# Decay attention feeding experts and a mish FFN: scores on two row halves of the array, state update by heads, tokens counted one step back

## The chip, the cores and the metric

One Trainium2 chip, of which the program uses one core. The metric is device time in microseconds (us). The engines are TensorE (PE, matmuls; its weight loads are listed as PEld), VectorE (DVE), ScalarE (ACT), GpSimd (POOL) and SyncE (SP, which here issues most DMAs). A trace gives busy spans and what each instruction waited for; L393 is line 393 of the kernel.

## What is computed

Three layers in a row, on 1536 tokens of 512 numbers, all float32. First a causal attention with a decay per head (2 sequences, 8 heads, 768 positions, head size 64), in its blocked form:

```python
for b in range(nb):
    intra = np.einsum('bhic,bhjc->bhij', qb, kb) * Dmask[None]
    intra = np.einsum('bhij,bhjd->bhid', intra, vb)
    inter = np.einsum('bhid,bhde->bhie', qb * lam_pow[None], kv_state)
    out[:, :, sl] = intra + inter
    kv_state = lam_block * kv_state + np.einsum('bhsd,bhse->bhde', kb * rev_pow, vb)
```

Then 8 experts, one for each token: the largest of 8 logits picks it, and its softmax probability weighs the token's result (relu MLP, 512 to 1024 to 512). Last a dense FFN, 512 to 2048 to 512, with h * tanh(softplus(h)) between.

## The kernel before

The attention runs as 12 steps (STEPS): 6 blocks of 128 positions, for each of the 2 sequences in turn. All engines' instructions stand in program order, which the Python loop `for i in range(NS)` (L553) writes out by hand; nothing reorders them. Iteration i of the loop does, in this order:

- load_step(i + 2): q and k transposed (qbd, k_t), k and v as they are (k_n, v_n), 256 KB each, by SP's queue, three buffers each;
- scores(i + 1): the score block a on PE (L393), then DVE's product pt with the decay table dec (L397);
- factors(i + 1) on POOL: kd, which is k by decay (L409), and qs, which is q by powers of lam (L415, L416); fade(i) on ACT: the old state faded (sl, L424);
- rows(i - 1): the attention output xt of the step before, turned into token rows r with 8 logits beside them (L474); pick(i - 1): the largest logit, its index, the one-hot oh_all (L501), the exponentials and their sum (L504);
- the low half of one expert weight piece on DVE (low, L194). A weight piece (128 x 1024) is split for the experts into a rounded high part (hi, ACT, L189) and the remainder (lo, DVE or POOL, L194);
- values(i): o, from the old state and qs (L433) and from v and pt (L442), is copied to xt by ACT (L446); u, the update of the state (L451); then place(i - 1): counts of tokens per expert in c on PE (L510, L511), the gate gt (L513, L514), the weighed rows xs on ACT (L517, L521), the slot of each token (jk, obs, slot_i, L523 to L527), and a scatter of the rows to the experts' bins by POOL (L533);
- update(i): DVE adds u to the faded state (L465);
- in iterations 1 to 8: the load and high half of the next weight piece (its low half comes an iteration later).

q lies in memory that is zero elsewhere: for each pair of heads the first head's q is on rows 0 to 63 of one half of qbd, the second's on rows 64 to 127 of the other half, so one matmul with the pair's k (128 rows) and 256 columns gives both heads' scores.

```python
PE.matmul(
    out=a[:, j, :].rearrange("p (a i) -> p a i", a=2), lhsT=k_t[:, hp, :], rhs=q[:, :, hp, :],
    start=True, stop=True)
```

A float32 matmul stands in the trace as two records, each with a weight load of its own. After the loop the last tokens are placed, and the first expert's tokens are put together directly on PE (spread, gather). Then come the experts (up, L719; down, L740 and L743; between them hh, L722 and L723; further splits by advance), and the FFN.

Of the kernel before, what the change touches and what calls it, by code (L numbers as in the profile page):

```python
# [11 lines left out]
F32 = mybir.dt.float32  # L12
# [48 lines left out]
def kernel(  # L61
# [58 lines left out]
    eps = const.tile([P, 1], F32, name="eps")  # L120
# [44 lines left out]
    with tc.manual_schedule():  # L165
# [104 lines left out]
        with ExitStack() as actx:  # L270
            ap = actx.enter_context(pool("attn"))

            qbd = []
            for i in range(3):
                t = ap.tile([P, 2, NP, P], F32, name=f"qbd{i}")
                qbd.append(t)
            DVE.memset(qbd[0][HD:P, 0], 0.0)
            DVE.memset(qbd[0][0:HD, 1], 0.0)
            for t in qbd[1:]:
                POOL.memset(t[0:HD, 1], 0.0)  # L280
                POOL.memset(t[HD:P, 0], 0.0)

# [41 lines left out]

            dec = ap.tile([P, NH, P], F32, name="dec")
            pw = ap.tile([P, NP, P], F32, name="pw")
# [4 lines left out]
            def decay(g):  # L331
                h = slice(4 * g, 4 * g + 4)
                DVE.tensor_copy(out=sc0[:, h, :], in_=lam_b[:, h].unsqueeze(2).to_broadcast([P, 4, P]))
# [5 lines left out]
            def powers():  # L339
                DVE.tensor_copy(out=sc0[:, 0:NP, :], in_=lam_p.unsqueeze(2).to_broadcast([P, NP, P]))  # L340
# [19 lines left out]
            POOL.memset(eps, 1e-9)  # L360
# [18 lines left out]
            pt, qs, kd, xt, sld, rk, us, direct = {}, {}, {}, {}, {}, {}, {}, {}  # L379
            NS = len(STEPS)  # L380

            def scores(i):
                if i >= NS:
                    return
                q, k_t, k_n, v_n = ld[i]
                n = STEPS[i][0]
                for g in range(2):
                    if i == 0:
                        decay(g)
                    a = ps.tile([P, 2, 2 * P], F32, tag="a", name=f"a{i}_{g}", bufs=3)  # L390
                    for j in range(2):
                        hp = 2 * g + j
                        PE.matmul(  # L393
                            out=a[:, j, :].rearrange("p (a i) -> p a i", a=2), lhsT=k_t[:, hp, :], rhs=q[:, :, hp, :],
                            start=True, stop=True)
                    t = ap.tile([P, 4, P], F32, tag="pt", name=f"pt{i}_{g}", bufs=4)
                    DVE.tensor_tensor(  # L397
                        out=t.rearrange("p h i -> p (h i)"), in0=a.rearrange("p h i -> p (h i)"),
                        in1=dec[:, 4 * g:4 * g + 4, :].rearrange("p h i -> p (h i)"), op=ALU.mult)
                    pt[i, g] = t  # L400

            def factors(i):
# [4 lines left out]
                if n < NCH - 1:  # L407
# [3 lines left out]
                        in1=dec[:, :, P - 1:P].to_broadcast([P, NH, HD]), op=ALU.mult)  # L411
# [15 lines left out]
            def values(i):  # L427
# [10 lines left out]
                for h in range(NH):  # L438
                    if h == NH // 2 and i == NS - 2:
                        place(i - 1)  # L440
# [3 lines left out]
                        rhs=pt[i, hp // 2][:, h % 4, :], start=(n == 0 and hp == 0), stop=True, skip_group_check=True)  # L444
# [3 lines left out]
                if n < NCH - 1:  # L448
                    u = us[i] = ps.tile([P, NP, P], F32, tag="u", name=f"u{i}", bufs=1)
                    for hp in range(NP):  # L450
                        PE.matmul(  # L451
                            out=u[:, hp, :], lhsT=kd[i][:, 2 * hp:2 * hp + 2, :].rearrange("p h d -> p (h d)"),
                            rhs=v_n[:, hp * P:(hp + 1) * P], start=True, stop=True)
                if 1 <= i < NS - 2:
                    place(i - 1)

            def update(i):
                n, b = STEPS[i]
                if n < NCH - 1:
                    for z in range(2):  # L460
                        r = slice(z * HD, (z + 1) * HD)
                        if n == 0:
                            DVE.tensor_copy(out=state[b][r, :, r], in_=us[i][r, :, r])
                        else:
                            DVE.tensor_tensor(  # L465
                                out=state[b][r, :, r], in0=us[i][r, :, r], in1=sld[i][r, :, r], op=ALU.add)
# [21 lines left out]
            def pick(i):  # L488
# [9 lines left out]
                DVE.tensor_scalar(out=nm, in0=m8[:, 0:1], scalar1=-1.0, scalar2=None, op0=ALU.mult)  # L498
# [6 lines left out]
                rk[i] = (rv, sm)  # L505

            def place(i):
                rv, sm = rk.pop(i)
                c = ps.tile([P, NE], F32, tag="c", name=f"c{i}", bufs=1)
                PE.matmul(out=c, lhsT=tri[:, 1, :], rhs=obs, start=True, stop=False)  # L510
                PE.matmul(out=c, lhsT=tri[:, 0, :], rhs=oh_all[:, i, :], start=False, stop=True)  # L511
# [3 lines left out]
                xs = ap.tile([P, NP, P], F32, tag="xs", name=f"xs{i}", bufs=2)  # L515
# [491 lines left out]
```

## Time and profile before

| | |
|---|---|
| median of 3 runs (lowest to highest) | 542.11 us (541.7 to 542.39) |
| profiled execution: time, span | 541.75 us, 540.1 us |
| PE busy, share of the span | 522.6 us, 97% |
| PEld | 451.4 us, 84% |
| DVE | 369.8 us, 68% |
| ACT | 324.7 us, 60% |
| POOL | 185.2 us, 34% |
| granted TensorE clock, mean | 0.994 |

The shares are averages over three stages. The attention loop ends at about 85 us, the experts follow, then the FFN. A busy PE need not be a PE at its peak, since the ends of matmuls are modelled; the distance between the starts of blocks tells more.

### The profile page before, as it was taken

Reading aid. Unit: us, or ns where it says so; the run is one execution under the profiler, and the core shown is the slowest. Engines: PE = TensorE matmul, PEld = TensorE weight load, DVE = VectorE, ACT = ScalarE, POOL = GpSimd, SP = SyncE. Lnnn points to the kernel's source line nnn. Section 1 sums busy time; section 2 is a strip of 40 time slices with the busy share of each in tenths; the row PEclk is TensorE's granted clock in tenths of the full one; section 3 lists DMA queues with packets and bytes.
Section 4 is the critical chain, followed back from the end, with each engine's and each line's share of the span. In section 5 each row is a group of like instructions: output and inputs, shape, how many; then the busy total and the mean of one; then the engine's idle time right before and its main releaser. Section 6 shows DMA issues by size and latency. Waiting matters only on the chain. (4 is left out here: it accounts for less than half of the span.)

```text
span 540.1 us, 8441 instructions
## 1 busy us (share of the span) xinstructions
PE 522.6 (97%) x3101; PEld 451.4 (84%) x3102; DVE 369.8 (68%) x668; ACT 324.7 (60%) x514; POOL 185.2 (34%) x151
## 2 busy tenths in 40 slices
PE   8999988999999999999999999999999999999993
PEld 5888878999999999999788878888888888888882
DVE  7999965765967858653498776567965778436362
ACT  1566533655674566555678876777666775765650
POOL 7788842755573331235100321003210031103032
PEclk9999999999999999999999999999999999999997
DMA  8999837119999996731301024020230000001022
GB/s 259 340 329 332 277 147 292 52 49 399 315 299 224 223 360 236 262 128 40 118 0 62 18 79 133 23 79 0 95 139 4 0 0 1 0 1 58 21 80 81
DMA packets 28944, 74.98 MB, mean 139 GB/s; under 512 B 6652, under 2 KB 6652, under 8 KB 28896
## 3 DMA queue, kind: packets, MB, share of 16 engines
q1 hardware_dynamic: 25040, 66.62, 38.3%
q0 software_dynamic: 3424, 7.23, 3.6%
q8 instruction: 26, 0.43, 0.4%
q10 hardware_dynamic: 432, 0.53, 0.3%
q14 instruction: 22, 0.18, 0.1%
HBM read 66.61 MB, written 10.49 MB: 143 GB/s over the span
## 5 line engine op out<-in xcount | busy, mean ns | idle before, releaser
L194 POOL TENSOR_TENSOR lo_f<-w,hi_f 128x1024 fp32r<-128x1024 f32 x16 | 39.8, 2487 | 185.9 <-ACT hi_f L189 155.1
L719 PE MATMUL h<-x,hi_w 128*128 128x232 f32 x512 | 87.5, 274 | 0.0
L740 PE MATMUL y<-hh,hi_w 128*128 128x464 f32 x256 | 84.8, 380 | 0.9 <-DVE hh L723 0.9
L796 PE MATMUL hp<-yt,hi_f 128*128 128x512 f32 x256 | 79.3, 391 | 0.0
L719 PEld LDWEIGHTS h<-x,hi_w 128*128 128x128 f32 x512 | 77.8, 192 | 0.0
L828 PE MATMUL acc<-hi_f,ghi 128*128 128x512 f32 x192 | 76.2, 397 | 0.4 <-ACT Y L833 0.4
L828 PE MATMUL acc<-hi_f,glo 128*128 128x512 f32 x192 | 75.8, 395 | 0.0
L828 PE MATMUL acc<-lo_f,ghi 128*128 128x512 f32 x192 | 75.7, 394 | 0.0
L136 DVE TENSOR_TENSOR t<-t,hp 128x512 f32<-128x512 f32 x48 | 32.8, 684 | 61.1 <-ACT t L135 61.1
L719 PE MATMUL h<-x,lo_w 128*128 128x232 f32 x256 | 71.1, 278 | 0.0
L743 PE MATMUL y<-hh,lo_w 128*128 128x232 f32 x256 | 69.1, 270 | 0.0
L194 DVE TENSOR_TENSOR lo_w<-raw,hi_w 128x1024 fp32r<-128x1024 f32 x50 | 63.0, 1283 | 7.5 <-ACT hi_w L189 6.9
L132 ACT ACTIVATE t<-hp 128x512 f32<-128x512 f32 x48 | 28.6, 600 | 62.4 <-PE hp L796 62.1
L189 ACT ACTIVATE hi_w<-raw 128x1024 fp32r<-128x1024 f32 x64 | 64.5, 1055 | 0.9 <-DMA raw<-in_w1p_dram 0.9
L194 POOL TENSOR_TENSOR lo_w<-raw,hi_w 128x1024 fp32r<-128x1024 f32 x14 | 35.1, 2510 | 71.5 <-ACT hi_w L189 70.8
L796 PEld LDWEIGHTS hp<-yt,hi_f 128*128 128x128 f32 x256 | 48.1, 188 | 11.1
L740 PEld LDWEIGHTS y<-hh,hi_w 128*128 128x128 f32 x256 | 48.2, 188 | 6.1 <-DVE hh L723 1.1
L796 PE MATMUL hp<-yt,lo_f 128*128 128x512 f32 x128 | 50.4, 394 | 0.0
L719 PEld LDWEIGHTS h<-x,lo_w 128*128 128x128 f32 x256 | 49.0, 191 | 0.5
L743 PEld LDWEIGHTS y<-hh,lo_w 128*128 128x128 f32 x256 | 48.9, 191 | 0.0
L722 ACT ACTIVATE hh<-h 128x464 fp32r<-128x464 f32 x32 | 17.8, 558 | 49.7 <-PE h L719 45.2
L723 DVE SCALAR_TENSOR_TENSOR hh<-h,hh 128x464 fp32r<-128x464 f32 x32 | 20.4, 639 | 34.8 <-ACT hh L722 34.8
(163 smaller groups left out, 1032.9 us busy)
## 6 DMA issues: line engine op xcount, KB each, us to landing
raw<-in_w1p_dram SPq DMA_DIRECT2D x32, 512.0 KB
raw<-in_w2p_dram SPq DMA_DIRECT2D x32, 512.0 KB
w<-in_w3p_dram SPq DMA_DIRECT2D x32, 512.0 KB
xw<-bins SPq DMA_DIRECT2D x7, 512.0 KB
qbd<-in_qT_dram SPq DMA_DIRECT2D x24, 128.0 KB
v_n<-in_vN_dram SPq DMA_DIRECT2D x12, 256.0 KB
k_n<-in_kN_dram SPq DMA_DIRECT2D x10, 256.0 KB
k_t<-in_kT_dram SPq DMA_DIRECT2D x10, 256.0 KB
```

Source lines behind the costliest of these rows:

```text
L132: yield lambda: ACT.activation(out=t, in_=h, func=AF.Tanh, scale=0.5)
L136: yield lambda: DVE.tensor_tensor(out=t, in0=t, in1=h, op=ALU.mult)
L189: ACT.activation(out=hi, in_=r, func=AF.Copy)
L194: engine.tensor_tensor(out=lo, in0=r, in1=hi.bitcast(F32), op=ALU.subtract)
L719: PE.matmul(out=p[:, m, :], lhsT=w[:, s], rhs=x[k // 2][:, k % 2, r, :], start=(k == 0 and m == 0 and z == 0), stop=(k == KD - 1 and z == ...
L722: ACT.activation(out=h[:, :, 0, :], in_=p, func=AF.Relu)
L723: DVE.scalar_tensor_tensor(out=h[:, :, 1, :], in0=p, scalar=0.0, in1=h[:, :, 0, :].bitcast(F32), op0=ALU.max, op1=ALU.subtract)
L740: PE.matmul(out=y.rearrange("p z n -> p (z n)"), lhsT=whi[:, s], rhs=h[:, f].rearrange("p z n -> p (z n)"), start=(c == 0 and f == 0), sto ...
L743: PE.matmul(out=y[:, 1, :], lhsT=wlo[:, s], rhs=h[:, f, 0, :], start=False, stop=(c == 3 and f == 1), skip_group_check=True)
L796: PE.matmul(out=p, lhsT=w[:, s], rhs=x, start=(k == 0 and z == 0), stop=(k == KD - 1 and z == 2))
L828: PE.matmul(out=acc[t], lhsT=x[:, s], rhs=w[:, DM:2 * DM], start=(first and z == 0), stop=(last and z == 2))
```

## The change

- q is loaded as it is, in one DMA, without the zeroed halves (which six memsets had cleared). The scores of a pair of heads are two matmuls: the first head on rows 0 to 63, the second on rows 64 to 127, each 128 columns, into two score tiles, one for each place in the pair. The decay table is ordered by place in the pair to match. POOL's sum of the two halves of q (L415) goes.
- The state update u is computed by heads: 8 matmuls of 64 by 64 instead of 4 of 128 by 128, of which only the diagonal blocks were used.
- place is split in three: weigh (gate and xs), locate (c, jk, obs, slot_i) and scatter. weigh(i - 1) stands ahead of values(i); locate and scatter come one step later, for i - 2, behind the next scores and the next factors.
- The negation nm and the addition of 1e-9 to the sum go from DVE to ACT. kd reads the last column of the decay table from a copy (last).
- Weight pieces are split in iterations 3 to 8 instead of 1 to 8; the two that are missing are split when the experts begin. Iterations 9 and 10 load three pieces each instead of two.

```diff
             def load_qk(i, queue):
-                q = qbd[i % 3]
+                q = ap.tile([P, NP, P], F32, tag="q", name=f"q{i}", bufs=3)
                 k_t = ap.tile([P, NP, P], F32, tag="k_t", name=f"k_t{i}", bufs=3)
                 queue.dma_start(out=k_t, in_=kT[i])
-                SP.dma_start(out=q[0:HD, 0], in_=qT[i, 0:HD])
-                SP.dma_start(out=q[HD:P, 1], in_=qT[i, HD:P])
+                SP.dma_start(out=q, in_=qT[i])
...
             def powers():
+                DVE.tensor_copy(
+                    out=last.rearrange("p (h z) -> p h z", z=2),
+                    in_=dec.rearrange("p (z h) i -> p h z i", z=2)[:, :, :, P - 1])
...
-                for g in range(2):
+
+                a = [ps.tile([P, NP, P], F32, tag="a", name=f"a{i}_{z}", bufs=3) for z in range(2)]
+                for hp in range(NP):
+                    for z in range(2):
+                        r = slice(z * HD, (z + 1) * HD)
+                        PE.matmul(out=a[z][:, hp, :], lhsT=k_t[r, hp, :], rhs=q[r, hp, :], start=True, stop=True)
+                for z in range(2):
                     if i == 0:
-                        decay(g)
-                    a = ps.tile([P, 2, 2 * P], F32, tag="a", name=f"a{i}_{g}", bufs=3)
...
                 if n > 0:
                     s = ap.tile([P, NP, P], F32, tag="qs", name=f"qs{i}", bufs=2)
-                    POOL.tensor_tensor(out=s, in0=q[:, 0], in1=q[:, 1], op=ALU.add)
-                    POOL.tensor_tensor(out=s, in0=s, in1=pw, op=ALU.mult)
+                    POOL.tensor_tensor(out=s, in0=q, in1=pw, op=ALU.mult)
...
-                    u = us[i] = ps.tile([P, NP, P], F32, tag="u", name=f"u{i}", bufs=1)
-                    for hp in range(NP):
+                    u = us[i] = ps.tile([P, NP, HD], F32, tag="u", name=f"u{i}", bufs=1)
+                    for h in range(NH):
+                        hp, z = divmod(h, 2)
                         PE.matmul(
-                            out=u[:, hp, :], lhsT=kd[i][:, 2 * hp:2 * hp + 2, :].rearrange("p h d -> p (h d)"),
-                            rhs=v_n[:, hp * P:(hp + 1) * P], start=True, stop=True)
-                if 1 <= i < NS - 2:
-                    place(i - 1)
+                            out=u[z * HD:(z + 1) * HD, hp, :], lhsT=kd[i][:, h, :],
+                            rhs=v_n[:, h * HD:(h + 1) * HD], start=True, stop=True)
...
-                DVE.tensor_scalar(out=nm, in0=m8[:, 0:1], scalar1=-1.0, scalar2=None, op0=ALU.mult)
+                ACT.activation(out=nm, in_=m8[:, 0:1], func=AF.Copy, scale=-1.0)
...
-                DVE.tensor_scalar(out=gt, in0=sm, scalar1=eps[:, 0:1], scalar2=None, op0=ALU.add)
+                ACT.activation(out=gt, in_=sm, func=AF.Copy, bias=1e-9)
...
                 scores(i + 1)
+                if 2 <= i < NS - 1:
+                    locate(i - 2)
                 if i == 0:
                     powers()
                     factors(0)
                 factors(i + 1)
+                if 2 <= i < NS - 1:
+                    scatter(i - 2)
                 fade(i)
...
                 late = []
+                if 1 <= i < NS - 1:
+                    weigh(i - 1)
                 values(i)
+                if i == NS - 2:
+                    locate(i - 1)
+                    scatter(i - 1)
                 if i == 0:
                     constants()
                 update(i)
-                if 1 <= i <= 8:
+                if 3 <= i <= 8:
                     p, r = next_raw()
                     pieces[p] = high(r, f"w{p}")
                     late.append((p, r))
                 if i in (9, 10):
-                    for _ in range(2):
+                    for _ in range(3):
                         load_piece()
```

How the instructions stand on three engines, in iteration 6 of the loop. A row is a line, an operation and its tiles; the first number in a tile's name is the step it belongs to.

PE before: the scores a7, the rows r5, the output o6 (old state, then values), the update u6, the counts c5.

```order
L393 MATMUL a7_0_700<-qbd1_108,k_t7_603 128x256 x2
L393 MATMUL a7_1_705<-qbd1_108,k_t7_603 128x256 x2
L474 MATMUL r5_0_720<-rw_151,xt5_664 128x136 x3
L474 MATMUL r5_1_721<-rw_151,xt5_664 128x136
L433 MATMUL o6_740<-qs6_623,state0_158 128x128 x4
L442 MATMUL o6_740<-pt6_0_614,v_n6_518 64x128 x4
L442 MATMUL o6_740<-pt6_1_619,v_n6_518 64x128 x4
L451 MATMUL u6_755<-v_n6_518,kd6_621 128x128 x4
L510 LDWEIGHTS tri_63
L510 MATMUL c5_760<-obs_67,tri_63 128x8
L511 LDWEIGHTS tri_63
L511 MATMUL c5_760<-oh_all_66,tri_63 128x8
```

PE with the change: the first three rows are the last of eight score matmuls of step 7, and the last two the first of eight value matmuls of step 6, behind which the eight of u6 follow.

```order
L385 MATMUL a7_0_718<-q7_612,k_t7_613 128x128
L385 MATMUL a7_1_719<-q7_612,k_t7_613 128x128
L511 LDWEIGHTS tri_63
L511 MATMUL c4_732<-obs_67,tri_63 128x8
L512 LDWEIGHTS tri_63
L512 MATMUL c4_732<-oh_all_66,tri_63 128x8
L463 MATMUL r5_0_749<-rw_141,xt5_690 128x136 x3
L463 MATMUL r5_1_750<-rw_141,xt5_690 128x136
L425 MATMUL o6_775<-qs6_643,state0_149 128x128 x4
L432 MATMUL o6_775<-pt6_0_630,v_n6_518 64x128
L432 MATMUL o6_775<-pt6_1_632,v_n6_518 64x128
```

The scores alternate between two tiles, and the counts have moved from behind u to behind the scores, for the token tile one step further back.

DVE before, from the one-hot of tile 5 to the first logits of tile 6 (obs is the running count, dec the decay table):

```order
L501 TENSOR_SCALAR oh_all_66<-iota8_64,i85_733 128x8
L194 TENSOR_TENSOR lo_w4_690<-raw4_509,hi_w4_689 128x1024
L513 TENSOR_SCALAR gt5_763<-sm5_737,eps_90 128x1
L514 RECIPROCAL gt5_763<-gt5_763 128x1
L523 SCALAR_TENSOR_TENSOR jk5_769,slot_f_68<-c5_760,oh_all_66 128x8
L526 TENSOR_TENSOR obs_67<-obs_67,oh_all_66 128x8
L527 CAST slot_i_69<-slot_f_68 128x1
L465 TENSOR_TENSOR state0_158<-u6_755,sl6_715 64x4x64 x2
L397 TENSOR_TENSOR pt8_0_792<-a8_0_789,dec_153 128x512
L397 TENSOR_TENSOR pt8_1_797<-a8_1_794,dec_153 128x512
L492 TENSOR_REDUCE lg6_815<-r6_0_809 128x8
```

DVE with the change, between the same two places:

```order
L490 TENSOR_SCALAR oh_all_66<-iota8_64,i85_762 128x8
L193 TENSOR_TENSOR lo_w2_708<-raw2_607,hi_w2_707 128x1024
L500 RECIPROCAL gt5_768<-gt5_768 128x1
L454 TENSOR_TENSOR state0_149<-u6_790,sl6_744 64x4x64 x2
L390 TENSOR_TENSOR pt8_0_824<-a8_0_814,dec_143 128x512
L390 TENSOR_TENSOR pt8_1_826<-a8_1_815,dec_143 128x512
L514 SCALAR_TENSOR_TENSOR jk5_831,slot_f_68<-c5_828,oh_all_66 128x8
L517 TENSOR_TENSOR obs_67<-obs_67,oh_all_66 128x8
L518 CAST slot_i_69<-slot_f_68 128x1
L481 TENSOR_REDUCE lg6_851<-r6_0_845 128x8
```

Negation (which stood ahead of this piece) and addition are gone, the reciprocal (gt) stands directly behind the split lo, and jk, obs and slot_i have moved behind the next pt products.

POOL before, between two scatters (DMA rows):

```order
L533 DMA bins_60<-xs4_677,slot_i_69 12288x512
L409 TENSOR_TENSOR kd7_710<-k_n7_609,dec_153 128x512
L415 TENSOR_TENSOR qs7_712<-qbd1_108 128x512
L416 TENSOR_TENSOR qs7_712<-qs7_712,pw_154 128x512
L533 DMA bins_60<-xs5_766,slot_i_69 12288x512
```

POOL with the change:

```order
L526 DMA bins_60<-xs3_576,slot_i_69 12288x512
L402 TENSOR_TENSOR kd7_739<-k_n7_618,last_144 128x512
L408 TENSOR_TENSOR qs7_741<-q7_612,pw_145 128x512
L526 DMA bins_60<-xs4_674,slot_i_69 12288x512
L402 TENSOR_TENSOR kd8_835<-k_n8_716,last_144 128x512
```

One product of q remains of two operations, and the scatter is that of one tile further back.

## Rows read from the trace of the kernel before

**Rows 1.** View by windows (PE, PEld, DVE, ACT, POOL busy us; clock, DMA share, GB/s).

```profile
36.74:69.47 32.73, 31.33 (x252) 26.35 (x251) 30.92 (x91) 19.33 (x50) 27.70 (x20) 1.00 0.95 309
...
100.00:540.10 440.10, 430.73 (x2395) 373.05 (x2393) 286.69 (x418) 279.48 (x405) 116.72 (x66) 0.99 0.34 109
```

**Rows 2.** Timeline of DVE, one step: start us, us, instruction.

```profile
36.50 1.21 DVE L194 TENSOR_TENSOR lo_w<-raw,hi_w 128x1024 fp32r<-128x1024 f32 x1
37.64 0.20 DVE L513 TENSOR_SCALAR gt<-sm,eps 128x1 f32<-128x1 f32 x1
...
38.02 0.83 DVE L526 TENSOR_TENSOR obs<-obs,oh_all 128x8 bf16<-128x8 bf16 x1
...
41.60 0.15 DVE L498 TENSOR_SCALAR nm<-m 128x1 f32<-128x1 f32 x1
...
41.94 1.13 DVE L501 TENSOR_SCALAR oh_all<-iota,i 128x8 bf16<-128x8 f32 x1
42.98 1.21 DVE L194 TENSOR_TENSOR lo_w<-raw,hi_w 128x1024 fp32r<-128x1024 f32 x1
```

**Rows 3.** Timeline of POOL, the same step.

```profile
36.63 2.20 POOL L416 TENSOR_TENSOR qs<-qs,pw 128x512 f32<-128x512 f32 x1
...
41.76 1.27 POOL L415 TENSOR_TENSOR qs<-qbd 128x512 f32<-128x512 f32 x1
```

**Rows 4.** Timeline of DVE, 69 to 75 us.

```profile
70.75 0.16 DVE L526 TENSOR_TENSOR obs<-obs,oh_all 128x8 bf16<-128x8 bf16 x1
...
74.04 0.23 DVE L501 TENSOR_SCALAR oh_all<-iota,i 128x8 bf16<-128x8 f32 x1
```

**Rows 5.** Timeline of PE, the step of rows 2.

```profile
36.74 1.97 PE L393 MATMUL a<-qbd,k_t 128*128 128x256 f32 x8
38.70 1.19 PE L474 MATMUL r<-rw,xt 128*128 128x136 f32 x8
39.73 1.05 PE L433 MATMUL o<-qs,state 128*128 128x128 f32 x8
40.72 1.09 PE L442 MATMUL o<-pt,v_n 128*64 128x128 f32 x16
41.74 1.16 PE L451 MATMUL u<-v_n,kd 128*128 128x128 f32 x8
42.74 0.17 PE L510 MATMUL c<-obs,tri 128*128 128x8 bf16 x1
```

**Rows 6.** Timeline of PE, 12.6 to 18.6 us.

```profile
12.70 1.89 PE L393 MATMUL a<-qbd,k_t 128*128 128x256 f32 x8
14.43 1.09 PE L474 MATMUL r<-rw,xt 128*128 128x136 f32 x8
```

**Rows 7.** Waits, 12.7 to 87 us: who for whom, us in total, times, longest.

```profile
PEld u L451 <- issue: 1.5, 9, 0.2
...
PEld a L393 <- DMA qbd<-in_qT_dram: 0.7, 2, 0.4
```

**Rows 8.** Timeline of PE, row matmuls of token tiles 1 and 10.

```profile
20.43 1.09 PE L474 MATMUL r<-rw,xt 128*128 128x136 f32 x8
...
76.63 1.09 PE L474 MATMUL r<-rw,xt 128*128 128x136 f32 x8
```

**Rows 9.** Timeline of ACT, 75 to 100 us, the tail.

```profile
75.61 0.60 ACT L446 ACTIVATE xt<-o 128x512 f32<-128x512 f32 x1
...
79.82 0.36 ACT L521 ACTIVATE xs<-r,gt 128x128 f32<-128x128 f32 x1
```

**Rows 10.** Timelines of DVE, PE and ACT, the first experts.

```profile
97.68 2.29 DVE L194 TENSOR_TENSOR lo_w<-raw,hi_w 128x1024 fp32r<-128x1024 f32 x2
99.89 0.63 DVE L723 SCALAR_TENSOR_TENSOR hh<-h,hh 128x464 fp32r<-128x464 f32 x1
...
93.57 0.48 PE L740 MATMUL y<-hh,hi_w 128*128 128x464 f32 x1 [0.91 <-DVE hh L723]
...
99.14 0.56 ACT L722 ACTIVATE hh<-h 128x464 fp32r<-128x464 f32 x1 [2.39 <-PE h L719]
```

More of the change, by code (lines that the diff above doesn't have):

```diff
@@ L271 @@
             ap = actx.enter_context(pool("attn"))
[L273 to L281, printed above, removed]
             make_identity(nc, ident)
@@ L325 @@
             dec = ap.tile([P, NH, P], F32, name="dec")
+            lam_z = lam_b.rearrange("p (h z) -> p z h", z=2)
+            last = ap.tile([P, NH], F32, name="last")
             pw = ap.tile([P, NP, P], F32, name="pw")
@@ L386, in scores @@
                 n = STEPS[i][0]
-                for g in range(2):
-                    if i == 0:
-                        decay(g)
-                    a = ps.tile([P, 2, 2 * P], F32, tag="a", name=f"a{i}_{g}", bufs=3)
[L391 to L396, printed above, removed]
+                a = [ps.tile([P, NP, P], F32, tag="a", name=f"a{i}_{z}", bufs=3) for z in range(2)]
[4 more added lines that the diff above has]
+                for z in range(2):
+                    if i == 0:
+                        decay(z)
+                    t = ap.tile([P, NP, P], F32, tag="pt", name=f"pt{i}_{z}", bufs=4)
                     DVE.tensor_tensor(
-                        out=t.rearrange("p h i -> p (h i)"), in0=a.rearrange("p h i -> p (h i)"),
-                        in1=dec[:, 4 * g:4 * g + 4, :].rearrange("p h i -> p (h i)"), op=ALU.mult)
-                    pt[i, g] = t
+                        out=t.rearrange("p h i -> p (h i)"), in0=a[z].rearrange("p h i -> p (h i)"),
+                        in1=dec[:, 4 * z:4 * z + 4, :].rearrange("p h i -> p (h i)"), op=ALU.mult)
+                    pt[i, z] = t
             def factors(i):
@@ L462, in update @@
                         if n == 0:
-                            DVE.tensor_copy(out=state[b][r, :, r], in_=us[i][r, :, r])
+                            DVE.tensor_copy(out=state[b][r, :, r], in_=us[i][r])
                         else:
                             DVE.tensor_tensor(
-                                out=state[b][r, :, r], in0=us[i][r, :, r], in1=sld[i][r, :, r], op=ALU.add)
+                                out=state[b][r, :, r], in0=us[i][r], in1=sld[i][r, :, r], op=ALU.add)
             def rows(i):
@@ L504, in pick, with weigh @@
                 ACT.activation(out=ex, in_=lg, func=AF.Exp, bias=nm[:, 0:1], accum_out=sm)
[L505 to L511, printed above, removed]
                 gt = ap.tile([P, 1], F32, tag="gt", name=f"gt{i}", bufs=2)
-                DVE.tensor_scalar(out=gt, in0=sm, scalar1=eps[:, 0:1], scalar2=None, op0=ALU.add)
+                ACT.activation(out=gt, in_=sm, func=AF.Copy, bias=1e-9)
+                rk[i] = (rv, gt)
+            def weigh(i):
+                rv, gt = rk.pop(i)
                 DVE.reciprocal(out=gt, in_=gt)
-                xs = ap.tile([P, NP, P], F32, tag="xs", name=f"xs{i}", bufs=2)
+                xs = xg[i] = ap.tile([P, NP, P], F32, tag="xs", name=f"xs{i}", bufs=3)
                 n = rv[0].shape[1]
@@ L521, in place, with locate @@
                     ACT.activation(out=xs[:, n:NP], in_=rv[1], func=AF.Copy, scale=gt[:, 0:1])
+            def locate(i):
+                c = ps.tile([P, NE], F32, tag="c", name=f"c{i}", bufs=1)
+                PE.matmul(out=c, lhsT=tri[:, 1, :], rhs=obs, start=True, stop=False)
+                PE.matmul(out=c, lhsT=tri[:, 0, :], rhs=oh_all[:, i, :], start=False, stop=True)
                 jk = ap.tile([P, NE], F32, tag="jk", name=f"jk{i}", bufs=1)
```

21 lines of the change are left out of this document (11 added, 10 removed).

## The prediction

> **What bounds the kernel now.** I read the stages first, in the view by windows. From 100 us to the end TensorE (PE) is busy 430.73 of 440.10 us, so whatever is gained before the experts start should reach the end nearly whole. In the attention loop, 36.74 to 69.47 us, PE and VectorE (DVE) are both about 95% busy and the DMA engines stand at 0.95: three candidates [rows 1]. Shares don't decide between them; one step does.
>
> The DVE timeline of one step decides it. From one weight split (lo, 36.50) to the next (42.98) is 6.48 us, and every DVE operation starts as the one ahead ends [rows 2]. Two of them are far too long for 8 elements: the one-hot (oh_all) takes 1.13 us and the counter (obs) 0.83 us. The POOL timeline says why: the first ends at 43.07, when POOL's sum of the two q halves ends (41.76 + 1.27), and the second at 38.85, when POOL's product qs ends (36.63 + 2.20) [rows 3]. Where POOL runs no such operation beside them, the same two take 0.23 and 0.16 us [rows 4]. DVE is therefore the bound, and about a quarter of its step is waiting for POOL.
>
> PE only looks as full: its blocks in this step start 1.96, 1.03, 0.99, 1.02 and 1.00 us apart (scores a, rows r, old state into o, values into o, state update u), and c fills the rest of 6.48 [rows 5]. The score block is stretched, because the r behind it waits for the evacuation xs, which waits for DVE. At the start of the loop the same block of 8 records takes 14.43 - 12.70 = 1.73 us [rows 6]. Unstretched, PE needs 1.73 + 1.03 + 0.99 + 1.02 + 1.00 + 0.25 (c without its wait, an estimate) = 6.0 us.
>
> **The change, part by part.** All times are against the profiled execution: span 540.1, time 541.75, which is 0.36 below the median 542.11.
>
> *DVE and POOL.* The sum of the q halves goes from POOL (1.27 us a step), and with it the cause of the long one-hot: 1.13 becomes 0.23. The counter moves behind the next step's pt, by when kd and qs should be over: 0.83 becomes 0.16. Negation (0.15) and the small addition (0.20) go to ScalarE (ACT). DVE's step falls to 6.48 - 0.90 - 0.67 - 0.35 = 4.6 us, and in the first two steps that used to carry a split (1.21) by that more. What is late next is PE.
>
> *PE.* The scores become 8 matmuls of 64 rows by 128 columns, 16 records instead of 8 of twice the columns. No row of before has half-height matmuls. Nearest is the values block: also 16 records of 128 columns, its weights alternating between two halves of the array (by columns), started 1.02 us apart from the next block. The other end is that the halves don't share: the rows block has 8 records of full width in 1.03, so 16 take 2.06 [rows 5]. I take 1.02, since the values block is alike in count, type and alternation; both ends stay for the range. The state update becomes 16 records of half width: by the same row 1.02, no gain (below it could go to about half, 0.5; above, 16 at the rows block's pace, 2.06, which its column halves make unlikely). One more point: u's weights wait 1.5 us in 9 steps, 0.17 each, for nothing that the trace shows, just where the array goes from half-width to full-width blocks [rows 7]. Before, a step has two such changes of shape (into the values, out of them); after, three (into the values, from u to the scores, from the scores to c). I add 0.17. The Trainium skill, TensorEngine Tiling (Array Packing), Key Properties, says that a change of tiling mode drains the engine. It gives no price; the trace agrees with 0.17 us at one such place.
>
> PE's step: 1.02 + 0.25 + 1.03 + 0.99 + 1.02 + 1.02 + 0.17 = 5.5 us.
>
> *The loop through ACT.* r of one step must be summed, picked, weighed (xs) and the next xt copied behind it before the next r. At the tail, without a split, r starts at 76.63 and the second xs ends at 79.82 + 0.36 = 80.18; the xt copy takes 0.60 [rows 8, 9]. That is 4.15 us, and with a split of 1.21 ahead of the reciprocal 5.4. The two small ACT operations replace two of DVE in this chain, at about the same length. It lies just under PE's 5.5, so I take a step of 5.65, with 0.15 for the two getting in each other's way.
>
> *The sum.* From r of token tile 0 (14.43) to that of tile 1 (20.43) is 6.00 now, partly c waiting for the one-hot; after it PE's blocks without old state are 1.03 + 1.02 + 1.02 + 0.17 + 1.02 + 0.25 = 4.5: **1.5 gained**. From r of tile 1 (20.43) to r of tile 10 (76.63) is 56.2 now; after it eight steps of 5.65 and a last one without split at the loop's 4.15 + 0.15 = 4.3, together 49.5: **6.7 gained**. In the tail the last xt stands behind a negation and an addition on ACT: **0.3 lost** (estimate: two operations like the 0.20 addition). Before 14.43 I take nothing: memsets go from POOL and DVE, but kd of tile 0 now waits for the column copy behind four pt products instead of the decay table alone; one microsecond either way is my choice.
>
> *The two splits in the experts* cost ACT two conversions and DVE 2.29 (the pair in [rows 10]) between the first two hh. I cost them at nothing. DVE's third hh would move from 99.89 to about 102.2. PE asks for it after one down and one up block more; down and up together took 99.14 - 93.57 = 5.6, so at about 104.7. If that cover were gone, PE would lose up to 2.3 us once.
>
> Sum: 1.5 + 6.7 - 0.3 = 7.9; 541.75 - 7.9 = 533.85, and with the 0.36 to the median **534.2 us**.
>
> **The rivals.**
>
> *DMA becomes the bound.* A step with a weight piece moves 4 x 256 KB of loads, 512 KB of weights and a 256 KB scatter, 1.84 MB; at the loop's 309 GB/s that is 5.95 us [rows 1], above 5.65. For it: scores already waited for q twice, 0.7 us [rows 7]. Against: the q of tile 7, which waited, now has three pieces (1.57 MB, 5.1 us) fewer ahead of it, about what compute gains by then. If DMA sets the six steps that carry a piece, 6 x 0.3 = 1.8 us of the gain go: 536.0.
>
> *The row halves don't overlap,* so the change doesn't do what it says on PE. The score block is 2.06, a step 6.5 to 6.6: over r of tile 1 to 10 8 x 6.55 + 5.0 = 57.4, 1.2 lost, against 0.5 won between the first two r and 0.3 lost in the tail: about 1 us longer, but for DVE's slack; 541 to 543, hardly to be told from no change. For it: no row shows half-height weights, and a load of 128 columns is twice that of the values block. Against: the values block does overlap its halves.
>
> *Slower: weight loads come out from under the multiplies.* Each half-height matmul is two records on the same rows; if the second record's weights had to wait for the first one's multiply, three loads and three multiplies in turn (two of eight hidden by the other half) at about 0.115 us make 0.7 us per head pair, 2.8 per block and 7.4 per step. From r of tile 1 to 10 that is 8 x 7.4 + 6 = 65 against 56.2, and with the first step and the tail 9.6 us longer: 551.7. It decides as soon as the block passes about 1.9 us, where the 7.9 us over nine or ten blocks are used up. Against it: the rows block does 8 loads and 8 multiplies on the same rows in 1.03 us, 0.13 a record, which leaves no room for taking turns [rows 5]. The Trainium skill, TensorE: Matmul & The Clock Gate, Part 3, says that a load overlaps a running multiply only where the row group differs; by that rule this rival would hold, and the trace's full-height blocks speak against the rule.
>
> **How the numbers follow.** The forecast (overlap, PE bound, 531 to 536) has 0.62; DMA bound or a partly shared score block, 536 to 540.5, 0.18; no overlap 0.13; slower by the weight loads 0.07. A measurement of this kernel can tell about 0.2%, 1.1 us, from no change. Faster takes the first two and a little of the third: 0.81. Same: most of the third, 0.10. Slower: 0.09. The lower end is the state update at half its block (0.5 a step, as far as the ACT loop lets it, about 0.15 x 8) and a start that wins 1 us: 531.5, rounded to 531. The upper end, 540.5, reaches over the partly shared cases up to the edge of no overlap; beyond it lie the 0.2 that are left out.
>
> **What would show it.** Right: score blocks of about 1.0 us, one-hot near 0.23 and obs near 0.16, PE's step 5.5 to 5.7 without gaps, DVE with idle time of up to 1 us, the first expert matmul about 8 us sooner, and the stage from there to the end as long as now. Wrong: score blocks near 2 us; a PE that waits for q in the middle steps; r waiting for xt by over 0.3 us a step; or an expert stage that starts 8 us sooner and ends less than that sooner, which would mean that its first hh, splits or scattered rows are late.

## The result, and the profile after

The changed kernel takes 536.98 us (median of 4 runs, 534.69 to 537.28) against 542.03 before (4 runs, 541.70 to 542.39): 0.9907 by the medians. The ratio on record, which the table below goes on with, is 0.9886, with a 95% interval of 0.9858 to 0.9915. It is faster by 5.1 us where 7.9 were forecast (534.2). The range, 531 to 540.5, held it, but in the part that the prediction gave to DMA or a partly shared score block, not in that of its own forecast (531 to 536). The profiled execution took 537.28 with a span of 535.6; its own stages, beside those of before and of the prediction's sum, show that the result is made of errors in both directions:

| stretch on PE | before | predicted | after |
|---|---|---|---|
| start to r of tile 1 | 20.43 | 18.9 | 21.28 |
| r of tile 1 to r of tile 10 | 56.20 | 49.5 | 47.34 |
| r of tile 10 to the first expert multiply (h) | 10.30 | 10.6 | 13.68 |
| from there to the end | 453.17 | 453.2 | 453.30 |

The loop won 8.9 us and the two ends gave 4.2 back.

**The step.** Timeline of PE after, one step (start us, us, instruction, idle time before it):

```profile
34.02 0.64 PE L442 MATMUL u<-v_n,kd 128*64 128x64 f32 x16
34.58 1.16 PE L385 MATMUL a<-q,k_t 64*128 64x128 f32 x16
35.68 0.18 PE L511 MATMUL c<-obs,tri 128*128 128x8 bf16 x1
...
36.16 1.20 PE L463 MATMUL r<-rw,xt 128*128 128x136 f32 x8 [0.28 <-ACT xt L436]
37.20 1.05 PE L425 MATMUL o<-qs,state 128*128 128x128 f32 x8
38.18 1.09 PE L432 MATMUL o<-pt,v_n 128*64 128x128 f32 x16
39.10 0.63 PE L442 MATMUL u<-v_n,kd 128*64 128x64 f32 x16
41.03 1.16 PE L385 MATMUL a<-q,k_t 64*128 64x128 f32 x16 [1.30 <-DMA q<-in_qT_dram]
```

The score block takes 35.68 - 34.58 = 1.10 us, against 1.96 in [rows 5] and 1.73 unstretched in [rows 6]. u takes 0.56 in the steps where the next block starts at once (34.02 to 34.58), against 1.00. The step, 6.48 before, would be about 5.1 here; it is 6.45, because the next scores wait for q. On DVE, in the same step, the two operations that POOL had stretched in [rows 2] are short:

```profile
37.06 0.16 DVE L517 TENSOR_TENSOR obs<-obs,oh_all 128x8 bf16<-128x8 bf16 x1
...
38.21 0.23 DVE L490 TENSOR_SCALAR oh_all<-iota,i 128x8 bf16<-128x8 f32 x1
```

The one-hot stays short in the whole loop. The counter doesn't: in two of ten steps, those whose scores had waited for q, obs again runs beside POOL's qs, takes 1.21 and 1.22 us and ends with it (DVE and POOL):

```profile
43.48 1.21 DVE L517 TENSOR_TENSOR obs<-obs,oh_all 128x8 bf16<-128x8 bf16 x1
...
43.41 1.26 POOL L408 TENSOR_TENSOR qs<-q,pw 128x512 f32<-128x512 f32 x1
```

**The new bound.** Waits of PE after, 36 to 60 us (engine and line, for whom: us in total, times, longest), and below them the view by windows (stretch, then busy us of PE, PEld, DVE, ACT, POOL; granted clock, DMA share, GB/s):

```profile
PE a L385 <- DMA q<-in_qT_dram: 2.4, 2, 1.3
PE r L463 <- ACT xt L436: 1.7, 3, 1.1
```

```profile
40.30:56.52 16.22, 12.95 (x168) 11.89 (x170) 13.63 (x46) 11.43 (x33) 9.28 (x9) 1.00 1.02 385
100.00:535.60 435.60, 425.43 (x2351) 368.11 (x2349) 283.43 (x415) 276.09 (x401) 113.10 (x64) 0.99 0.34 110
12.00:20.00 8.00, 6.94 (x72) 6.36 (x72) 6.07 (x16) 1.18 (x6) 5.86 (x24) 0.57 0.63 230
72.00:84.00 12.00, 11.17 (x62) 10.19 (x63) 4.39 (x23) 2.74 (x9) 3.57 (x4) 0.72 0.76 265
```

From 40 to 56 us neither PE (80%) nor DVE (84%) is full; DMA is, at 385 GB/s against 309 in [rows 1]. In two other stretches PE's granted clock is 0.57 and 0.72 of 2.4 GHz, so PE ran at 1.2 GHz for part of them; before, the same stretches read:

```profile
12.00:20.00 8.00, 7.10 (x56) 6.29 (x55) 7.40 (x26) 2.13 (x6) 6.25 (x24) 1.00 1.04 350
72.00:84.00 12.00, 9.81 (x92) 8.53 (x91) 7.27 (x42) 4.27 (x13) 4.70 (x5) 1.00 0.39 145
```

**The two ends.** PE's timeline after, at the start and in the tail, shows a wait ahead of each of these stretches and blocks at twice their length behind it (the scores of tile 2 take 2.08 us, not 1.16):

```profile
13.06 1.12 PE L442 MATMUL u<-v_n,kd 128*64 128x64 f32 x16 [1.42 <-POOL kd L402]
14.11 2.08 PE L385 MATMUL a<-q,k_t 64*128 64x128 f32 x16
...
71.71 1.06 PE L471 MATMUL lg<-rw,xt 128*128 128x8 f32 x8 [0.87 <-ACT xt L436]
74.12 1.89 PE L538 MATMUL win_u<-hots,xs 128*128 128x232 f32 x4 [0.83 <-DVE m L485]
75.90 1.89 PE L538 MATMUL win_o<-hots,xs 128*128 128x232 f32 x4
```

Waits of the same length stood in the tail before, 0.70 and 0.83 us, and the clock held; why it falls here is open.

The wait ahead of u is the one the prediction saw coming: kd on POOL stands until the column copy "last" is done.

```profile
11.86 2.14 POOL L402 TENSOR_TENSOR kd<-k_n,last 128x512 f32<-128x512 f32 x2 [7.23 <-DVE last L331]
```

**The tokens' way.** Behind the loop, POOL's scatter of tile 9 must land before SP reads the first expert's rows ("first"); the next two scatters, the padding and the reads xw of the other experts' rows queue behind that. POOL and SP before, then after:

```profile
76.43 1.01 POOL L533 DMA_INDIRECT bins<-xs,slot_i  x1 [0.85 <-ACT xt L446]
...
79.34 0.38 SPq L585 DMA_DIRECT2D first<-bins  x1
```

```profile
68.83 0.96 POOL L526 DMA_INDIRECT bins<-xs,slot_i  x1 [1.55 <-ACT xt L436]
78.05 0.96 POOL L526 DMA_INDIRECT bins<-xs,slot_i  x1 [8.27 <-DMA first<-bins]
...
73.60 0.38 SPq L592 DMA_DIRECT2D first<-bins  x1
```

The read went out 2.9 us behind the scatter; now it is 4.8. The next scatter starts 4.4 to 4.5 us behind that read in every kernel here, whatever the view names as its releaser (4.44 before, 4.45 after), and ACT's first hh of the experts starts within about 0.4 us of SP's read of xw (92.28 and 92.56 before, 86.78 and 86.84 after). And at 119 us PE waits for the third expert's tokens, as it did not before (waits after, 100 to 125 us):

```profile
PE t L708 <- DMA xw<-bins: 1.3, 1, 1.3
```

### The profile page after: what moved, and what is told of

The parts are those of the page before. It is cut to its first block, busy times and chain, and to the rows that moved or that the text cites. A ratio compares the mean times of both kernels' runs of the same rounds, so it can differ in the third digit from the quotient of the medians.

```text
span 535.6 us, 8728 instructions
## 1 busy us (share of the span) xinstructions
PE 513.8 (96%) x3277; PEld 446.8 (83%) x3278; DVE 356.3 (67%) x643; ACT 328.5 (61%) x538; POOL 162.9 (30%) x136
## 4 chain that ended last, share of the span: by engine, by line
PE 79%; DMA 8%; issue 4%; DVE 3%; POOL 3%; ACT 2%; SPq 0%; POOLq 0%; ACTq 0%; DVEq 0%
PE acc L835 24%; PE hp L803 24%; PE h L726 13%; PE y L747 8%; PE y L750 4%; POOL bins L675 2%; DMA q<-in_qT_dram 2%; DMA xw<-bins 2%; DMA raw<-in_w1p_dram 1%; PE r L463 1%; PE a L385 1%; DMA bins<-zero,pad_i 1%; PE o L432 1%; DVE pt L390 1%; PE t L708 1%
## 5 line engine op out<-in xcount | busy, mean ns | idle before, releaser
L131 ACT ACTIVATE t<-hp 128x512 f32<-128x512 f32 x48 | 28.5, 598 | 62.4 <-PE hp L803 62.2
L835 PEld LDWEIGHTS acc<-hi_f,ghi 128*128 128x128 f32 x192 | 36.1, 188 | 9.3 <-ACT Y L840 1.1
```

The costliest lines, as they stand in the source:

```text
L131: yield lambda: ACT.activation(out=t, in_=h, func=AF.Tanh, scale=0.5)
L835: PE.matmul(out=acc[t], lhsT=x[:, s], rhs=w[:, DM:2 * DM], start=(first and z == 0), stop=(last and z == 2))
```

## The experiments

Theory: the matmul edits do what was forecast and more; the rest of the gain is lost (a) to q and k that DMA brings late, (b) at the start and in the tail to waits and the lower clock behind them, (c) to the tokens' way, which holds back the experts. The main rival is that a part of the change itself costs time. Each kernel is the changed one with the edit shown. The profiled executions by the stretches of the first table:

| kernel | median of all runs (range), us | ratio to before, 95% | profiled: start, loop, tail, rest |
|---|---|---|---|
| changed | 536.98 (534.69 to 537.28) | 0.9858 to 0.9915 | 21.28, 47.34, 13.68, 453.30 |
| e1 last column early | 536.33 (534.92 to 537.93) | 0.9878 to 0.9917 | 19.69, 47.17, 12.25, 454.2 |
| e2 idle multiplies in the tail | 536.34 (533.11 to 536.41) | 0.9836 to 0.9901 | 20.82, 49.31, 11.53, 453.0 |
| e3 token loads early | 535.35 (534.30 to 536.04) | 0.9857 to 0.9890 | 20.19, 47.03, 13.67, 451.7 |
| e4 heads grouped | 539.15 (534.74 to 539.77) | 0.9927 to 0.9960 | 20.50, 47.54, 10.99, 454.8 |
| e5 u in full | 538.46 (536.63 to 539.58) | 0.9890 to 0.9949 | 20.21, 49.33, 12.00, 456.3 |
| e6 splits and loads back | 532.77 (532.28 to 533.70) | 0.9807 to 0.9847 | 20.23, 47.16, 12.19, 451.5 |
| e7 loads early | 540.11 (535.86 to 541.25) | 0.9907 to 0.9967 | 20.97, 52.44, 12.24, 454.0 |
| e8 four edits together | 537.07 (535.45 to 540.96) | 0.9889 to 0.9951 | 19.68, 50.21, 11.96, 453.7 |
| e9 loads alone back | 533.91 (533.55 to 536.16) | 0.9822 to 0.9855 | 20.52, 48.50, 12.24, 453.1 |
| e10 POOL sum back | 538.73 (533.89 to 541.35) | 0.9843 to 0.9957 | 20.39, 53.91, 12.22, 453.2 |
| e11 count at once | 535.76 (534.99 to 536.23) | 0.9861 to 0.9894 | 20.06, 48.08, 13.63, 451.5 |
| e12 e6 and e1 | 532.67 (531.57 to 533.13) | 0.9806 to 0.9833 | 19.71, 47.71, 10.58, 452.9 |

Executions of one kernel lie up to 7.5 us apart here, and in e4 and e9 much of that goes with PE's granted clock, so totals 1 to 2 us apart tell little; the stretches and waits say more.

**e1, last column early.** The copy moves from powers() into scores(0):

```
 decay(z)
+if z == 1:
+    DVE.tensor_copy(out=last..., in_=dec...[:, :, :, P - 1])
```

> Edit: the copy of the last decay column is made right behind the decay table of the odd heads, ahead of the second product pt of tile 0, not behind four of them. Theory (the start lost 0.85 us because kd of tile 0 waits for this copy, PE stands 1.4 us before u of tile 0, and its granted clock falls to half right after): u of tile 0 starts within 0.5 us of the end of o, PE keeps 2.4 GHz through 12 to 19 us, r of tile 1 starts at 18 to 19.5 instead of 21.28, and the time falls by 1.5 to 3 us to about 534 to 535.5, unless the supply of tokens for the third expert (see the run of the early token loads) eats it. Rival (PE has too little to do here in any case, since pt and the loads of tile 1 are late as well): the clock falls as before, r of tile 1 moves by less than 0.7 us, the time by less than 0.8.

u of tile 0 starts at 11.42, without a wait, as expected. But PE's clock fell all the same, only earlier (granted 0.62 in 8 to 12 us), and r of tile 1 waits 1.7 us for its xt: it starts at 19.69, and the total can't be told from the change's. The wait was real, but it did not set the start alone: xt of tile 1 stands on ACT behind the xs of tile 0, in the order that the change gave them.

**e2, idle multiplies in the tail.**

```
+fill("c", 6)      # 6 multiplies 128x256 bf16
 rows(NS - 1)
 ...
+fill("u", 6)
 win = [ps.tile(...
```

> Edit: 6 multiplies of 128x256 bf16 that nobody reads, ahead of r of tile 11, and 6 more ahead of the first product with the one-hot window, where PE waits in the tail. Theory (the tail is 3.4 us longer than before because PE's granted clock falls to half after two waits of 0.8 us): the clock stays at 2.4 GHz from 72 to 80 us, from r of tile 10 to the first expert multiply 10.3 to 11.5 us instead of 13.68. If in addition the supply of tokens of the third expert is the cap on the gain, the wait for them (1.28 us at 119) grows by as much as the tail wins, 2 to 3 us, and the time stays within 0.7 us of the change's. Rival (no such cap): the time falls by 2 to 3 us. Second rival (PE's clock falls all the same, or the fillers come too late): tail within 0.7 us of 13.68.

Windows of e2:

```profile
72.00:84.00 12.00, 11.05 (x89) 9.61 (x84) 5.31 (x30) 4.18 (x14) 3.91 (x4) 1.00 0.73 251
```

The clock holds here and the tail is 2.15 us shorter, yet the median is within 0.7 us of the change's. In the profiled execution the loop takes back what the tail won: its granted clock is 0.72 from 54 to 60 us, behind a wait of 1.55 us for xt, and it is 2.0 us longer. So the total doesn't tell whether there is a cap. The waits show that another limit stands behind the tail: PE now waits 0.7 us for the first expert's rows and 1.4 for its first hh, though no more for tokens at 119. e4's tail, with the changed kernel's code and no fall, took 10.99: by that the fall costs 2.7 us of the 3.4. In e5, also with no fall there, the tail took 12.00, 1.2 of it a wait for the first expert's rows.

**e3, token loads early.**

```
-load_x(1)
 pad(2)
+load_x(1)
+load_x(2)
```

> Edit: the padding of the second expert and the loads of the tokens of experts 1 and 2 go together ahead of the other paddings, so that the load for expert 2 no longer waits for the last padding. Theory (this chain ends at 119 and stops PE there): the wait of 1.28 us at 119 is gone, first expert multiply to end 453.3 - 1.3 = 452.0, time about 1.2 us less. Rival (the wait is gone but what stands behind it, weights or splits, stops PE just after): the stretch from the first expert multiply to the end keeps its 453.3 within 0.4.

No wait is left between 100 and 125 us, and h to end fell from 453.3 to 451.7: (c) holds, at 1.6 us. The total is 1.6 lower too, within what the runs can tell.

**e4, heads grouped.**

```
-for hp in range(NP):
-    for z in range(2):
+for z in range(2):
+    for hp in range(NP):
```

> Edit: the four scores of the even heads are issued first, then the four of the odd heads, so that neighbours use the same half of the rows. Theory (the two row halves run beside each other because the heads alternate): the score block takes 1.7 to 2.06 us instead of 1.10; where DMA doesn't stop the step, it is 0.5 to 0.9 longer; in the steps at 40 to 56 us, where PE waits for q and k, nothing. Time 2 to 5 us longer. Rival (a record of 64 rows costs 0.065 us whatever its neighbour): block 1.0 to 1.2, time within 0.7 us of the change's.

PE of e4, the same step:

```profile
34.38 1.71 PE L385 MATMUL a<-q,k_t 64*128 64x128 f32 x16
36.02 0.18 PE L511 MATMUL c<-obs,tri 128*128 128x8 bf16 x1
```

1.64 us for the same 16 records: a little under the theory's 1.7, far from the rival's 1.2. The row halves run beside each other when neighbours alternate. The loop grew by only 0.2. The median rose by 2.2, as forecast, but that goes with the clock: two executions at a mean clock of 0.996 took 534.7 and 535.5, four at 0.981 to 0.989 took 539.0 to 539.8. The Trainium skill, TensorE: Matmul & The Clock Gate, Part 3, lets a weight load overlap a running multiply only where the row group differs; the order of 1.10 and 1.64 agrees. But 0.103 us a record on the same rows is still no taking of turns, as the rows block had said.

**e5, u in full.**

```
-for h in range(NH): ... lhsT=kd[i][:, h, :], rhs=v_n[:, h * HD:(h + 1) * HD]
+for hp in range(NP): ... lhsT=kd[i][:, 2 * hp:2 * hp + 2, :], rhs=v_n[:, hp * P:(hp + 1) * P]
```

> Edit: the state update again as 4 products of 128x128 per head pair, of which only the two diagonal blocks are read; all else as changed. Theory (by heads it is half the work: 0.56 to 0.6 us instead of the 1.02 that the prediction took): the block is 1.0 to 1.16 us again, steps that no DMA holds up take 5.1 to 5.6 instead of 4.7 to 5.1, and from r of tile 1 to r of tile 10 it is 1 to 2.5 us longer, less than 9 x 0.45 = 4, because DMA sets the steps at 40 to 56 us. Rival (by heads changes nothing but the records): within 0.5 us of the change's 47.34 over the same stretch.

```profile
28.51 1.16 PE L441 MATMUL u<-v_n,kd 128*128 128x128 f32 x8
29.60 1.16 PE L385 MATMUL a<-q,k_t 64*128 64x128 f32 x16
```

1.09 us against 0.56, unbound steps of 5.3, and 2.0 us more over the loop, as the theory had it. The rest is 3.0 us longer as well, which it did not have: PE waits 3.0 us for its first hh, and its clock falls at 90 to 94 us.

**e6, splits and loads back.**

```
-if 3 <= i <= 8:
+if 1 <= i <= 8:
 ...
-    for _ in range(3):
+    for _ in range(2):
         load_piece()
```

> Edit: eight weight splits in the loop, in steps 1 to 8, and two loads in steps 9 and 10, as before the change. Theory A (the move bought nothing much in the loop: DVE has idle time in every step, the pieces' loads are the same 8): r of tile 1 to tile 10 within 0.7 us of 47.34, r of tile 1 up to 1 us later, first y within 0.5 of the change's distance from the first h. Theory B (the splits take the bound in the steps they are in, about 1.2 us of ACT and of DVE ahead of xs and xt): r of tile 0 to tile 3 1.5 to 2.5 us longer, time 1 to 2.5 us more.

Neither theory had the result: the loop is as long as the change's (A), and the time is **4.2 us less**, below every run of the changed kernel. So the move of the two splits and their loads, which the prediction costed at nothing, cost 4.2 us, where the whole change won 5.1. POOL and SP of e6:

```profile
67.23 0.96 POOL L526 DMA_INDIRECT bins<-xs,slot_i  x1 [1.55 <-ACT xs L507]
74.61 0.96 POOL L526 DMA_INDIRECT bins<-xs,slot_i  x1 [6.42 <-ACT xs L503]
...
70.09 0.38 SPq L592 DMA_DIRECT2D first<-bins  x1
```

From scatter to read it is 2.9 us again, the next scatter starts 4.5 us behind the read as elsewhere, and PE waits neither for the first hh nor for tokens. With the two splits went their loads: six pieces of 512 KB (SP, 58.4 to 62.2 us) stood ahead of the scatter of tile 9 in the changed kernel, four in e6, which loads the other two early in the loop, where the DMA share was 0.63 (12 to 20 us). From 68 to 72 us, where that scatter's rows are on their way, the share is 0.75 in the changed kernel and 0.28 in e6. Not all of the 4.2 us need be the loads': by stretches, e6 is 1.8 us shorter in the rest, but also 1.1 in the start and 1.5 in the tail, where the changed kernel's clock was low for longer.

**e7, loads early.** Three pieces ahead of v of tile 3:

```
 load_qk(i, SP)
+if i == 3:
+    for _ in range(3): load_piece()
 load_vk(i, SP)
```

> Edit: three weight pieces are loaded right behind k and q of tile 3, ahead of the v loads that stand waiting for u of tile 0; before, these pieces came in later steps. Theory (DMA sets the steps at 40 to 56 us, while it stands at 0.3 to 0.4 around 14 to 20 us): the DMA share at 14 to 20 rises to 0.8 or more, the two waits for q of 1.30 and 1.14 us shrink to under 0.5 each, r of tile 1 to r of tile 10 falls from 47.3 to 45 to 46.3. Rival (the loads of tiles 2 and 3 are only pushed back): waits for k or v at 20 to 30 us take their place, the stretch stays within 0.5 of 47.3.

The share at 12 to 20 us rose to 1.03, but the rival held and more: PE waits 2.3 us for k_t there, one one-hot is stretched to 2.84 us (waits 24 to 60 us below), the clock falls three times (8 to 17, 35 to 41 and 79 to 83 us), and the loop takes 52.4. That q's lateness costs the changed kernel time (a) is thus read from its waits; no run here removes them and shows the gain.

```profile
PE c L515 <- DVE oh_all L493: 3.0, 1, 3.0
```

**e8, four edits together** (e1, e2, e3, e7, and 8 idle multiplies each ahead of o and r of tile 0).

> Edit: the early last column, the early token loads, the early piece loads and the idle multiplies in the tail together, and 8 such multiplies each ahead of o and of r of tile 0, where PE waits. Theory (start 1.5 to 2.5, loop 1 to 2, tail 2 to 3 and tokens 1.3 us add, but the first hh waits for the last scattered rows, so about 1 to 2 of it is lost again): granted clock 0.995 or more, first h at 75 to 78 us, time 530 to 533. Rival (the chain from the scattered rows eats it all): 534 or more.

537.07: the rival. Its parts don't add, with e7 among them, and the clock still falls in its loop (20 to 24 and 54 to 58 us).

**e9, loads alone back.** The pieces are loaded as in e6, the splits stay in the experts:

```
+if 1 <= i <= 8:
+    while n_load[0] <= min(2 * (i - 1), i + 1):
+        load_piece()
 if 3 <= i <= 8:
     p, r = next_raw()
```

> Edit: the weight pieces are loaded at the steps at which they were before the change (two of them earlier, two loads instead of three in steps 9 and 10), but the two splits stay in the experts. Theory L (putting the eight splits back won 4 us because of the loads: of the six late ones, two less stand ahead of the last scattered rows of the loop, so that the read of the first expert's rows goes out 2.9 us after its scatter and not 4.8): as fast as with the splits back, 532 to 534, the read of the first expert's rows at 69 to 71.5, no wait of PE for tokens near 119. Theory S (it won because the two splits are out of the way of the first expert): within 1 us of the change's 537.

533.91, in theory L's range, with an interval that lies just below the change's (0.9855 against 0.9858). The profiled execution is the slowest of the four (536.16; the others 533.55 to 534.04). It has the read 3.0 us behind the scatter, as L said, but at 71.9, after L's 71.5, and with a 1.3 us wait for tokens, which L excluded:

```profile
68.93 0.96 POOL L526 DMA_INDIRECT bins<-xs,slot_i  x1 [1.26 <-ACT xs L507]
...
71.94 0.38 SPq L595 DMA_DIRECT2D first<-bins  x1
```

By the medians 3.1 of the 4.2 us go with the loads; the last 1.1, the splits themselves, is not settled, as the intervals of e6 and e9 overlap. The traces show less. The profiled executions of e9 and of the changed kernel have nearly the same mean clock (0.982 and 0.983) and the scatter at the same time (68.93 and 68.83); e9's read comes 1.7 us sooner, its read of xw 1.1 sooner and its end 1.1 sooner. The other three executions of e9 ran at 0.992 to 0.994, the changed kernel's at 0.983 three times and at 0.988 once (534.69), e6's at 0.989 to 0.990. So a part of the 3.1 and of the 4.2, by these times an estimated 2 us of each, may be the clock's. Whether the place of the loads bears on the clock, no run here separates.

**e10, POOL sum back.**

```
+POOL.tensor_tensor(out=s, in0=q, in1=q, op=ALU.add)
 POOL.tensor_tensor(out=s, in0=q, in1=pw, op=ALU.mult)
```

> Edit: POOL sums two tensors of the size of q ahead of every product qs again (the result is overwritten). Theory (POOL's long operations hold small DVE operations up that run beside them): POOL's step grows by 1.27 us, the one-hot is 0.5 to 1.2 us in most steps instead of 0.23, and as DVE now has idle time and PE waits for q anyway, the time grows by only 0 to 2.5 us, less than the 9 x 0.9 = 8 that the one-hot cost before. Rival (the one-hot was long for another reason): it stays at 0.23 and the time within 0.7 us.

**e11, count at once.** locate(i - 2) and scatter(i - 2) go from the loop's head; behind values(i):

```
-if i == NS - 2:
+if 1 <= i < NS - 1:
     locate(i - 1)
     scatter(i - 1)
```

> Edit: the count of a tile's tokens and its scatter stand behind the state update of the next step again, not one step back. Theory (the counter was long because POOL's products ran beside it, and c waited for the one-hot): obs 0.3 to 1.3 us in most steps instead of 0.16, PE waits for c under 0.3 us a step, time 0 to 2 us more. Rival (counting earlier sends the scatter a step earlier, which takes it out of the way of the last one): the read of the first expert's rows goes out up to 2 us sooner, and the time is up to 2 us less than the change's 537.

A pair from e10 (DVE, POOL) and one from e11 show one mechanism on two victims:

```profile
42.17 1.09 DVE L518 TENSOR_TENSOR obs<-obs,oh_all 128x8 bf16<-128x8 bf16 x1
...
41.98 1.27 POOL L409 TENSOR_TENSOR qs<-q,pw 128x512 f32<-128x512 f32 x1
```

```profile
43.52 1.12 DVE L490 TENSOR_SCALAR oh_all<-iota,i 128x8 bf16<-128x8 f32 x1
...
43.33 1.27 POOL L408 TENSOR_TENSOR qs<-q,pw 128x512 f32<-128x512 f32 x1
```

Ends 43.26 and 43.25; 44.64 and 44.60: the small DVE operation ends when POOL's product does. In e10 the victim was mostly obs (median 1.1 us), not the one-hot; in e11 the one-hot (median 1.12), not obs. Which is hit depends on what falls beside qs, not on the operation. e10's total rose by 1.8, but its runs span 7.5 us; the loop of its profiled execution took 6.6 us more, with r waiting 6.7 us for xt, but also with a lower clock at 22 to 25 and 35 to 39 us, so that the 6.6 can't be put down to POOL alone. In e11 the total did not rise at all (535.76): r waits 5.3 us for xt there and not 2.3, but PE waits 0.6 for q and not 2.4, and the loop is 0.7 longer. Counting a step back bought no time that these runs can tell. The Trainium skill, SBUF — State Buffer, Who interferes with whom, says that a DVE operation that takes the port pair shared with GpSimd waits out the other's instruction; the ends agree, in the changed kernel's pair too (44.69 and 44.67).

**e12, e6 and e1 together.**

> Edit: the change with its eight splits and their loads back in steps 1 to 8, and with the last decay column copied early. Theory (the first removes 4.2 us of the change's 537.0, the second starts u of tile 0 within 0.3 us of the end of o and brings r of tile 1 from 20.2 to 19.7): 531.5 to 533, below the 532.8 of the splits alone by 0.3 to 1. Rival (the half microsecond at the start is lost in the steps that wait for q, which arrive when they arrive): 532.3 to 533.5, no different from the splits alone.

The rival: 532.67, no different from e6. It is the fastest kernel here with e6, 4.3 us below the changed one and 9.4 below the one before.

## Why the prediction was right, and where its steps failed

- **Scores, 1.02:** right, 1.10, which rules out both rivals of the row halves (2.06 and 2.8); e4 shows that the alternation makes it so.
- **DVE and POOL:** right in the main. The one-hot is 0.23, obs 0.16 in eight of ten steps and 1.2 in two, and DVE is no longer the bound; e10 and e11 bring the long ones back.
- **State update, 1.02:** mis-sized, 0.56. The values block was the wrong neighbour: it streams 128 columns, u by heads 64. The 0.5 end of the bounds was right.
- **Change of array shape, 0.17:** the scores start 0.56 us behind the first u record, which leaves no visible room for it.
- **PE's step, 5.5, and the ACT loop, 5.4 with a split:** both too long. Where nothing holds PE up, r follows r in 4.7 us (21.28 and 25.98); the step from r at 31.08 to r at 36.16 has a split in it and r waiting for xt at both ends, and took 5.1. This is why the loop gave 8.9 us, not the 6.7 of the forecast.
- **DMA as the bound:** the rival came true in two steps (scores at 34.58, 41.03 and 46.89: 6.45 and 5.86 us, where it had priced 5.95), inside a loop that was faster all the same. A third long step (scores at 52.03 and 57.88, 5.85 us) follows one with a stretched obs, and r waits 1.05 us for xt in it. PE waiting for q in the middle steps, and r for xt by over 0.3 us, were two of the prediction's signs of being wrong.
- **Start, 1.5 gained:** failed, 0.85 lost. The sum took PE's blocks alone, 4.5 from r of tile 0 to r of tile 1, and nothing ahead of them. r of tile 0 starts at 16.12 and not at 14.43 (kd did wait for the copy, and PE 1.4 us for kd), and from it to the next r is 5.2, at the lower clock. What sets 21.28 apart from the 20.1 to 20.2 of e3, e6 and e11, which keep the wait for kd, is the lower clock from 12 to 19 us. But 18.9 is not reached without either: in e8 and e12, which have neither, r of tile 1 starts at 19.7, as in e1, after a wait of 1.7 us for its xt, which ACT copies behind the xs of tile 0. The path through DVE and ACT is what the term left out.
- **Tail, 0.3 lost:** failed, 3.4 lost, 2.7 of it by the lower clock (e4); with no fall it took 10.99 in e4 and 10.58 in e12, where 10.6 was forecast. No term of the sum allowed for a clock.
- **"The two splits in the experts": costed at nothing, and of all the parts this is the one whose return wins most.** The splits were covered about as argued: PE's one wait there is for the first hh, which starts when SP's read of xw does, whether two splits stand behind it or not. It is 0.2 us after, when the slow tail hides it, 0.9 before, 1.2 in e12 and 1.4 to 3.0 in e2, e4 and e5. What was not followed is the loads that went with the splits: two pieces more behind the loop, ahead of the last scatter, so that the read behind it comes 1.9 us later. By the medians that is 3.1 us (e9), 4.2 with the splits (e6); 1.1 of it is followed through the traces, and a part of the rest may be the clock's.

So the side came out by a loop that was faster, for the reasons forecast and by the state update besides; only the update was put back alone (e5, 2.0 us of the loop), so the shares of the others in the 8.9 us are not shown. The size is luck: the loop's errors were favourable by 2.2 us, those of the start and the tail unfavourable by 2.4 and 3.1.

## What to carry to other kernels

When work moves, follow the transfers that it asks for onto every queue, up to the data that someone waits for behind them; here two loads of 512 KB, moved along with two splits, came to stand ahead of a scatter that the experts wait for, and by the medians they cost more than the splits. When an engine stops being the bound, recheck each "free" step against the new bound, which is DMA in the middle of the loop here. And measure each part of a change that is faster as a whole: the best kernel was the change less one of its parts.

## What was not expected of the hardware

PE's granted clock is not one number for a kernel whose PE has gaps: e4 ran at 534.7 to 535.5 us in the two executions with a mean of 0.996, and at 539.0 to 539.8 in the four with 0.981 to 0.989. In the profiled executions the falls to 1.2 GHz stood behind waits of 0.8 to 3 us, and never at the same place in all kernels. Such a wait is not enough, though: in the tail, the waits of 0.88 and 0.83 us of e4 and e12 and the 0.70 and 0.83 before had no fall behind them. What decides is not shown. The kernel before shows 1.00 in both stretches; its runs beside the change lie between 541.70 and 542.39, its runs beside the experiments between 541.44 and 545.20.
